# One lo part made by VectorE instead of TensorE, pair 1's weights widened in two steps, two convolution parts moved later, in a fused convolution and squared-ReLU MLP

## The chip, the cores and the metric

The kernel runs on one core of one Trainium2 chip. The metric is device time in microseconds (us), median of three runs: 2234.77 us before the change (2234.75 to 2234.77). The engines are TensorE (PE, with its weight loads PEld), VectorE (DVE), ScalarE (ACT), GpSimd (POOL) and SyncE (SP, which issues the DMAs). Each engine takes its own instructions in the order in which they stand, and waits for the others by semaphores.

## The reference

```
w   = exp(w - max(w)); w = w / (sum(w) + 1e-9)        # 8 heads x 7 taps, softmax over the taps
x   = causal convolution of x (8 x 4096 x 192) with w, head by head (24 channels each)
h   = x @ w_in            # 32768 x 192 @ 192 x 2048
g   = s * relu(h)**2 + b
out = g @ w_out           # 32768 x 2048 @ 2048 x 192
```

All of it is float32. w_in and w_out come to the core as 64-bit floats.

## The kernel before

**Precision.** TensorE works on fp32r, a rounded float32. Every factor is therefore split in a hi part (a cast to fp32r) and a lo part (the value minus its hi part), and a product is the sum of hi*hi, hi*lo and lo*hi. For an activation tile sA, slot 0 is hi and slot 1 is lo; W and WB hold the weights likewise.

**Tiling.** The 32768 tokens are 32 groups n of 1024, and a group is two blocks j of 512. The 192 channels are two parts: A (128 channels) and B (64 channels, those of both blocks stacked in one tile). The 2048 hidden units are eight pairs p of two chunks of 128. `first(n, j, p)` (L522) makes h for one pair: 18 matmuls of 64 rows each, two of which run side by side, with a PSUM tile h of which there are two. `relu` and `square` (L543, L551) on ACT, a cast for the hi part qh on ACT or DVE, and `lows` (L557) on DVE for the lo part ql follow. `second_whole` (n = 0, 10 matmuls) and `second` (later groups, 20 matmuls) multiply qh and ql by w_out and accumulate over the pairs. A queue holds at least two finished (qh, ql) back, so that TensorE runs `first` of later pairs ahead of `second` of earlier ones. At pairs 4 and 6 (`TWICE`) no second runs; pair 7 empties the queue.

**The convolution.** A group's convolution is a chain of small steps for DVE: seven taps (L161, L163) for A of block 0, then its split, seven for B (accB) with its split, and seven for A of block 1. `convolve(k)` (L708) emits the next k of these steps for the coming group; what a call leaves over where a tap chain ends is owed to the next call. For group 0 there is no earlier time: B and A of block 1 are convolved by TensorE with diagonal matrices (`conv_tensor`, L254), A of block 0 by DVE.

**The weights.** A pair's weights are widened from 64-bit words on the chip during group 0 (class `Widen`, L284): `magnitudes` (ACT, one instruction into a tile t, of which there are two), `top` (DVE, three instructions), `his` (ACT casts to the hi parts), `low` (DVE, two) and `los` (DVE, two for each part of the columns). Columns 0 to 383 are w_in of the pair, 384 to 767 its w_out. `fetch(p)` (L346) loads a pair's words by one DMA of 768 KB; there are three tiles of words, so `fetch(4)` waits until pair 1's words have been read.

**The order.** `head()` (L381) writes out the start by hand: group 0's convolution and splits, pair 0's weights (w_in and w_out apart), pair 1's, and the firsts of pairs 0 and 1 for both blocks with their squares, while pairs 2 and 3 are being widened. `pair(p)` (L724) does pairs 2 to 7 of group 0, widening pair p+2 and p+1 beside its own squares, with `CONV[p]` convolution steps of group 1. All of DVE, ACT and PE keep this written order over group 0 (`in_order`, L112; SP in `head` too). `ahead` and `between` in `pair` say how many of the steps come before and between the two blocks' squares. From group 1 on a plain loop over (n, j, p) runs (L777), with nothing of the weights left.

Of the kernel before, what the change touches and what calls it, by code (L numbers as in the profile page):

```python
# [9 lines left out]
F32 = mybir.dt.float32  # L10
F32R = mybir.dt.float32r
I32 = mybir.dt.int32
U32 = mybir.dt.uint32
AF = mybir.ActivationFunctionType
ALU = mybir.AluOpType
AX = mybir.AxisListType

P = 128
BLK = 512
# [1 line left out]

LAG = 2

CONV = (0, 1, 1, 1, 1, 1, 4, 8)

TWICE = (4, 6)

# [10 lines left out]
def conv_attention_then_squared_relu_mlp(  # L38
# [23 lines left out]
    nc = tc.nc  # L62
    D, T = outT.shape
    NPAIR = weights64.shape[0]
    K = taps.shape[2]
# [21 lines left out]
    raw = ctx.enter_context(tc.tile_pool(name="raw", bufs=2))  # L87
# [187 lines left out]
    def w_in(part, p, chunk, rows):  # L275
        return W[rows, p, part, chunk * P : (chunk + 1) * P]
# [4 lines left out]
    def w_outB(f, rows=slice(0, P)):  # L281
        return WB[rows, f // 2, f % 2, :]

    class Widen:  # L284


# [11 lines left out]
                yield (*(WB[:, self.p, :, k * DB : (k + 1) * DB] for k in range(2)), v)  # L298

        def magnitudes(self):  # L300
            self.t = raw.tile([P, CT], I32, name="t")[:, self.lo : self.hi]

            top = words[self.p][:, self.lo : self.hi, 1]
            nc.scalar.activation(self.t.bitcast(F32), top.bitcast(F32), AF.Abs)

        def top(self):
            t, top = self.t, words[self.p][:, self.lo : self.hi, 1]
            nc.vector.tensor_scalar(
                t.bitcast(F32), t.bitcast(F32), TOP_MIN, TOP_MAX, op0=ALU.max, op1=ALU.min
            )  # L310

            nc.vector.tensor_scalar(
                t, t, 3, 0x3FFFFFFF, op0=ALU.logical_shift_left, op1=ALU.bitwise_and
            )
            nc.vector.scalar_tensor_tensor(  # L315
                t, top, -0x40000000, t, op0=ALU.bitwise_and, op1=ALU.bitwise_or
            )
# [28 lines left out]
    def fetch(p, a=0, z=None):  # L346
        if a == 0:
            words[p] = wordp.tile([P, CT, 2], I32, name="words")
        z = z or CT
        nc.sync.dma_start(  # L350
            words[p][:, a:z].rearrange("p f w -> p (f w)"), w_words[p, :, 2 * a : 2 * z]
        )
# [10 lines left out]
    make_identity(nc, ident)  # L363

    nc.scalar.activation(tsum, idle[:, 0:2], AF.Exp)
    nc.vector.reduce_max(tmax, tap, axis=AX.X)
    nc.vector.tensor_tensor(
        tap, tap, tmax.unsqueeze(2).to_broadcast([P, 2, K]), op=ALU.subtract
    )
    nc.scalar.activation(tap, tap, AF.Exp)  # L370
    nc.vector.reduce_sum(tsum, tap, axis=AX.X)
    nc.vector.tensor_scalar(tsum, tsum, 1e-9, None, op0=ALU.add)
    nc.vector.reciprocal(tsum, tsum)
    nc.vector.tensor_tensor(tap, tap, tsum.unsqueeze(2).to_broadcast([P, 2, K]), op=ALU.mult)
# [6 lines left out]
    def head():  # L381


        one = tok[0]

        warm = ps_o.tile([P, BLK], F32, name="acc1")
        for cols in WARM:
            nc.tensor.matmul(
                warm[:, 0:cols], idle, idle[:, 0:1].to_broadcast([P, cols]), start=True, stop=True
            )  # L390
        w0, w0out, w1 = Widen(0, 0, CI), Widen(0, CI, CT), wide[1]

        def diagonal(w):
            d = act.tile([P, 2, BLK], F32, name="q").rearrange("p a (k f) -> p (a k) f", f=P)
            for k in range(K):
                nc.scalar.activation(d[:, k, :], ident, AF.Identity, scale=w[:, k : k + 1])
            return d

        top, bottom = slice(0, DB), slice(DB, P)
        diagB = diagonal(tapB)  # L400
        accB = ps_o.tile([P, BLK], F32, name="acc2")
        acc1 = ps_o.tile([P, BLK], F32, name="acc1")
        one.conv_tensor(accB, diagB, one.xB)
        acc0 = xs.tile([P, BLK], F32, name="accA")
        for _ in one.conv(acc0, one.xA, tapA, BLK):
            pass
        nc.scalar.mul(minus, ident, -1.0)
        diagA = diagonal(tapA)
        w0.magnitudes()
        split = one.split_A(0, acc0)  # L410
        next(split)
        w0.top()
        w0.his()
        tB = one.tB = xs.tile([P, 2, BLK], F32R, name="tB")
        wB = one.wB = xs.tile([P, 2, BLK], F32R, name="wB")
        hiB = xs.tile([P, BLK], F32R, name="hiB", bufs=1)
        lo = one.split_tensor(accB, hiB, lambda: one.conv_tensor(acc1, diagA, one.xA[:, BLK:], range(0, 2)))
        one.conv_tensor(acc1, diagA, one.xA[:, BLK:], range(2, K))
        next(split)
        fetch(2)  # L420
        w1.magnitudes()
        w0.rest()
        w1.top()
        nc.scalar.copy(tB[top, 0, :], hiB[top].bitcast(F32))
        nc.scalar.copy(wB[bottom, 0, :], hiB[top].bitcast(F32))
        lo(tB[bottom, 0, :], top)
        lo(wB[top, 0, :], top)
        w1.his()
        w1.low()
        w0out.magnitudes()  # L430
        w0out.top()
        w1.los()
        nc.scalar.copy(tB[top, 1, :], hiB[bottom].bitcast(F32))

        def second_block():
            sA = one.sA[1] = xs.tile([P, 2, BLK], F32R, name="sA", bufs=3)
            wA = one.wA[1] = xs.tile([P, 2, BLK], F32R, name="wA", bufs=3)
            lo1 = one.split_tensor(acc1, sA[:, 0, :])
            one.swap(wA[:, 0, :], sA[:, 0, :])
            lo(tB[bottom, 1, :], bottom)  # L440
            one.swap(wB[:, 1, :], tB[:, 1, :])
            lo1(sA[:, 1, :], slice(0, P))
            one.swap(wA[:, 1, :], sA[:, 1, :])


        ha = first(0, 0, 0, second_block)
        w0out.his()
        q = relu(ha)
        w0out.rest()
        wide[2].magnitudes()  # L450
        wide[2].top()
        fetch(3)
        start_tokens(1)
        fetch(4)
        ha = first(0, 0, 1)
        a1 = relu(ha)
        queue.append((0, 0, 0, *lows(*square(q, nc.vector.tensor_copy))))
        hb = first(0, 1, 0)
        wide[2].low()
        b0 = squares(hb, nc.scalar.copy)  # L460
        queue.append((0, 1, 0, *lows(*b0)))
        wide[2].his()
        wide[2].los()
        hb = first(0, 1, 1)
        queue.append((0, 0, 1, *lows(*square(a1, nc.scalar.copy))))
        wide[3].magnitudes()
        wide[3].top()
        b1 = squares(hb, nc.scalar.copy)
        wide[3].his()
        queue.append((0, 1, 1, *lows(*b1)))  # L470
        convolve(CONV[1])

    wide = {p: Widen(p, 0, CT) for p in range(1, NPAIR)}
# [48 lines left out]
    def first(n, j, p, meanwhile=None):  # L522
        h = ps_h.tile([P, 2, BLK], F32, name="h")
        halves = [tok[n].half(j, i) for i in range(2)]

        def both(w, part, at, start, stop):

            for i in range(2):
                chunk = halves[i][at]
                rows = slice(i * HB, (i + 1) * HB)  # L530
                nc.tensor.matmul(  # L531
                    h[:, i, :], w_in(w, p, chunk[0], rows), chunk[part], start=start, stop=stop
                )
# [315 lines left out]
```

## Time and profile before

| | |
|---|---|
| median of three runs | 2234.77 us |
| span of the profiled execution (first to last instruction) | 2232.9 us |
| what lies around the span | 1.9 us |
| PE busy | 2226.4 us, 100% of the span |
| DVE busy | 1753.5 us, 79% |
| ACT busy | 1286.4 us, 58% |
| granted TensorE clock | 1.00 in the whole span |
| chain that ended last | PE 98%, DVE 1%, ACT 1% |

The busy share is an average over stages: group 0 takes the first 90 us or so, and in the first four of the page's 40 slices DVE is at 8, 8, 9 and 8 tenths, later mostly at 7. An idle gap on PE before an instruction is shown in brackets with what ended it.

### The profile page before, as it was taken

Reading aid. Unit: us, or ns where it says so; the run is one execution under the profiler, and the core shown is the slowest. Engines: PE = TensorE matmul, PEld = TensorE weight load, DVE = VectorE, ACT = ScalarE, POOL = GpSimd, SP = SyncE. Lnnn points to the kernel's source line nnn. Section 1 sums busy time; section 2 is a strip of 40 time slices with the busy share of each in tenths; the row PEclk is TensorE's granted clock in tenths of the full one; section 3 lists DMA queues with packets and bytes.
Section 4 is the critical chain, followed back from the end, with each engine's and each line's share of the span. In section 5 each row is a group of like instructions: output and inputs, shape, how many; then the busy total and the mean of one; then the engine's idle time right before and its main releaser. Section 6 shows DMA issues by size and latency. Waiting matters only on the chain.

```text
span 2232.9 us, 45081 instructions
## 1 busy us (share of the span) xinstructions
PE 2226.4 (100%) x19330; PEld 1829.1 (82%) x19330; DVE 1753.5 (79%) x1995; ACT 1286.4 (58%) x1410; POOL 317.8 (14%) x205
## 2 busy tenths in 40 slices
PE   9999999999999999999999999999999999999999
PEld 6788888888888888888888888888888888888887
DVE  8898778777787787777877878778777787787764
ACT  8755555655555555555555555555655555556554
POOL 0022101111011011110110111111101111011110
PEclk9999999999999999999999999999999999999999
DMA  5113112121121111211111111112121121111110
GB/s 180 34 43 87 40 46 62 48 58 44 44 58 53 53 44 45 56 53 53 43 51 50 53 53 53 48 43 62 51 55 44 44 58 53 53 44 42 46 39 17
DMA packets 46168, 117.51 MB, mean 53 GB/s; under 512 B 7760, under 2 KB 8016, under 8 KB 45968
## 3 DMA queue, kind: packets, MB, share of 16 engines
q1 hardware_dynamic: 45824, 114.50, 18.6%
q8 instruction: 151, 2.47, 0.5%
q14 instruction: 49, 0.40, 0.1%
q10 hardware_dynamic: 144, 0.13, 0.0%
HBM read 31.64 MB, written 25.17 MB: 25 GB/s over the span
## 4 chain that ended last, share of the span: by engine, by line
PE 98%; DVE 1%; ACT 1%; DMA 0%; issue 0%; SPq 0%; DVEq 0%
PE acc L614 50%; PE h L531 46%; DVE accA L163 0%; PE acc L576 0%; ACT q L552 0%; DVE ql L559 0%; PE acc L577 0%; PE acc L583 0%; PE acc L582 0%; PE acc L581 0%; ACT qh L554 0%; ACT q L545 0%; DMA xA<-in_xA 0%; DVE t L315 0%; ACT oC L589 0%
## 5 line engine op out<-in xcount | busy, mean ns | idle before, releaser
L545 ACT ACTIVATE q<-h 128x1024 f32<-128x1024 f32 x512 | 525.5, 1026 | 902.8 <-PE h L531 900.4
L559 DVE TENSOR_TENSOR ql<-q,qh 128x1024 fp32r<-128x1024 f32 x512 | 656.7, 1283 | 56.3 <-ACT qh L554 2.6
L554 DVE CAST qh<-q 128x1024 fp32r<-128x1024 f32 x497 | 370.1, 745 | 395.7 <-ACT q L552 393.3
L614 PE MATMUL acc<-qh,W 64*128 64x512 f32 x3960 | 609.9, 386 | 0.0
L552 ACT ACTIVATE q<-q 128x1024 f32<-128x1024 f32 x512 | 543.6, 1062 | 15.9
L614 PEld LDWEIGHTS acc<-qh,W 64*128 64x128 f32 x3960 | 370.9, 184 | 77.9
L531 PE MATMUL h<-sA,W 64*128 64x512 f32 x3072 | 432.4, 387 | 0.0
L531 PE MATMUL h<-wA,W 64*128 64x512 f32 x3072 | 431.6, 386 | 0.0
L531 PE MATMUL h<-tB,W 64*128 64x512 f32 x1536 | 429.9, 386 | 0.0
L531 PE MATMUL h<-wB,W 64*128 64x512 f32 x1536 | 429.9, 386 | 0.0
L614 PE MATMUL acc<-ql,WB 64*128 64x512 f32 x1980 | 385.7, 386 | 0.4 <-DVE ql L559 0.4
L614 PE MATMUL acc<-qh,WB 64*128 64x512 f32 x1980 | 385.6, 386 | 0.0
L614 PE MATMUL acc<-ql,W 64*128 64x512 f32 x1980 | 385.5, 386 | 0.0
L638 POOL TENSOR_TENSOR oB<-oB,oB 128x512 f32<-128x512 f32 x61 | 115.2, 1889 | 1672.7 <-ACT oB L637 1672.7
L163 DVE SCALAR_TENSOR_TENSOR accA<-xA,tap,accA 128x512 f32<-128x512 f32 x378 | 341.5, 903 | 6.8
L531 PEld LDWEIGHTS h<-sA,W 64*128 64x128 f32 x3072 | 287.3, 184 | 62.9 <-issue 1.1
L531 PEld LDWEIGHTS h<-wA,W 64*128 64x128 f32 x3072 | 287.8, 184 | 60.4
L531 PEld LDWEIGHTS h<-tB,W 64*128 64x128 f32 x1536 | 282.6, 184 | 40.5 <-issue 0.2
L531 PEld LDWEIGHTS h<-wB,W 64*128 64x128 f32 x1536 | 282.5, 184 | 20.1
L614 PEld LDWEIGHTS acc<-ql,WB 64*128 64x128 f32 x1980 | 185.5, 184 | 40.1 <-DVE ql L559 1.3
L614 PEld LDWEIGHTS acc<-ql,W 64*128 64x128 f32 x1980 | 185.5, 184 | 39.0
L614 PEld LDWEIGHTS acc<-qh,WB 64*128 64x128 f32 x1980 | 185.5, 184 | 38.8
(115 smaller groups left out, 1035.4 us busy)
## 6 DMA issues: line engine op xcount, KB each, us to landing
wA<-sA SPq DMA_DIRECT2D x126, 256.0 KB, 3.6
outT<-oA SPq DMA_DIRECT2D x63, 256.0 KB, 2.0
wB<-tB SPq DMA_DIRECT2D x60, 256.0 KB, 3.4
xA<-in_xA SPq DMA_DIRECT2D x24, 515.0 KB, 3.6
xB<-in_xB SPq DMA_DIRECT2D x32, 259.0 KB, 2.6
oC<-oB SPq DMA_DIRECT2D x61, 128.0 KB, 2.2
outT<-oC SPq DMA_DIRECT2D x60, 128.0 KB, 2.3
words<-in_w SPq DMA_DIRECT2D x7, 768.0 KB, 6.2
```

The lines of the kernel that those rows point to most:

```text
L163: nc.vector.scalar_tensor_tensor(acc, src, w[:, k : k + 1], acc, op0=ALU.mult, op1=ALU.add)
L531: nc.tensor.matmul(h[:, i, :], w_in(w, p, chunk[0], rows), chunk[part], start=start, stop=stop)
L545: nc.scalar.activation(q, h, AF.Relu)
L552: nc.scalar.activation(q, q, AF.Square)
L554: cast(qh, q)
L559: nc.vector.tensor_tensor(ql, q, qh.bitcast(F32), op=ALU.subtract)
L614: nc.tensor.matmul(accs[to + 2 * i], w(f, r), q[r, f % 2, :], start=start and f == 0, stop=stop and f == ends[i],)
L638: nc.gpsimd.tensor_tensor(o[1], o[1], o[3], op=ALU.add)
```

## The change

Five things change, all of them in group 0.

1. The tap softmax: the maximum comes negated, and two ACT exponentials (one for each part) take it as a bias and give the sums as well. A DVE subtraction and a DVE sum are gone.
2. In `head`, ACT casts hiB before W's hi part of pair 0 (`w0.his()` moved behind `split_tensor`).
3. Block 1's first lo part, acc1 minus its hi part: was a matmul with minus the identity between the third and fourth group of `first(0, 0, 0)` and an ACT copy out of PSUM; is one DVE subtraction that reads PSUM, and stands ahead of `first(0, 0, 0)`. The DMAs that swap halves stand in another order.
4. Pair 1's weights: w_in is widened where the whole pair was, w_out later, behind the first three squares, ahead of pair 3's. `fetch(4)` moves behind it. Pair 2's magnitudes and top move behind `first(0, 0, 1)` and the first ql.
5. `CONV` goes from (0, 1, 1, 1, 1, 1, 4, 8) to (0, 0, 0, 1, 1, 1, 5, 9).

```diff
-CONV = (0, 1, 1, 1, 1, 1, 4, 8)
+CONV = (0, 0, 0, 1, 1, 1, 5, 9)
...
         def magnitudes(self):
-            self.t = raw.tile([P, CT], I32, name="t")[:, self.lo : self.hi]
+            t = raws[self.p] = raw.tile([P, CT], I32, name="t")
+            self.t = t[:, self.lo : self.hi]
...
+        def part(self, lo, hi):
+
+            of = Widen(self.p, lo, hi)
+            of.t = raws[self.p][:, lo:hi]
+            return of
...
-    nc.vector.reduce_max(tmax, tap, axis=AX.X)
-    nc.vector.tensor_tensor(
-        tap, tap, tmax.unsqueeze(2).to_broadcast([P, 2, K]), op=ALU.subtract
-    )
-    nc.scalar.activation(tap, tap, AF.Exp)
-    nc.vector.reduce_sum(tsum, tap, axis=AX.X)
+    nc.vector.reduce_max(tmax, tap, axis=AX.X, negate=True)
+    for g in range(2):
+        nc.scalar.activation(
+            tap[:, g, :], tap[:, g, :], AF.Exp, bias=tmax[:, g : g + 1],
+            accum_out=tsum[:, g : g + 1],
+        )
...
         w0.top()
-        w0.his()
...
         lo = one.split_tensor(accB, hiB, lambda: one.conv_tensor(acc1, diagA, one.xA[:, BLK:], range(0, 2)))
+        w0.his()
...
-        w1.magnitudes()
+        wide[1].magnitudes()
+        w1, w1out = wide[1].part(0, CI), wide[1].part(CI, CT)
         w0.rest()
-        w1.top()
...
+        w1.top()
         w1.his()
         w1.low()
+        w1.los()
         w0out.magnitudes()
+        nc.scalar.copy(tB[top, 1, :], hiB[bottom].bitcast(F32))
+        lo(tB[bottom, 1, :], bottom)
+        one.swap(wB[:, 1, :], tB[:, 1, :])
...
+        nc.scalar.copy(sA[:, 0, :], acc1)
+        one.swap(wA[:, 0, :], sA[:, 0, :])
         w0out.top()
-        w1.los()
...
-            lo1 = one.split_tensor(acc1, sA[:, 0, :])
...
-            lo1(sA[:, 1, :], slice(0, P))
...
-        ha = first(0, 0, 0, second_block)
+        nc.vector.tensor_tensor(
+            sA[:, 1, :], acc1, sA[:, 0, :].bitcast(F32), op=ALU.subtract
+        )
+        one.swap(wA[:, 1, :], sA[:, 1, :])
+
+        ha = first(0, 0, 0)
         w0out.his()
         q = relu(ha)
         w0out.rest()
-        wide[2].magnitudes()
-        wide[2].top()
         fetch(3)
         start_tokens(1)
-        fetch(4)
         ha = first(0, 0, 1)
-        a1 = relu(ha)
         queue.append((0, 0, 0, *lows(*square(q, nc.vector.tensor_copy))))
+        a1 = relu(ha)
+        wide[2].magnitudes()
+        wide[2].top()
...
         queue.append((0, 0, 1, *lows(*square(a1, nc.scalar.copy))))
+        w1out.top()
+        w1out.his()
+        w1out.rest()
+        fetch(4)
+        b1 = relu(hb)
         wide[3].magnitudes()
+        b1 = square(b1, nc.scalar.copy)
         wide[3].top()
-        b1 = squares(hb, nc.scalar.copy)
```

The order on ACT about the relu of `first(0, 1, 1)`. q_365 before and q_367 after are that relu's tile; t_262 and t_289 belong to pair 2, t_360 and t_369 to pair 3, t_190 to pair 1.

Before:

```order
L322 CAST W_96<-t_262 128x640
L322 CAST WB_97<-t_262 128x2x64
L552 ACTIVATE q_294<-q_294 128x1024
L554 CAST qh_356<-q_294 128x1024
L304 ACTIVATE t_360<-words_267 128x768
L545 ACTIVATE q_365<-h_336 128x1024
L552 ACTIVATE q_365<-q_365 128x1024
```

After:

```order
L331 CAST W_96<-t_289 128x640
L331 CAST WB_97<-t_289 128x2x64
L565 ACTIVATE q_287<-q_287 128x1024
L567 CAST qh_349<-q_287 128x1024
L331 CAST W_96<-t_190 128x256
L331 CAST WB_97<-t_190 128x2x64
L558 ACTIVATE q_367<-h_329 128x1024
L307 ACTIVATE t_369<-words_257 128x768
L565 ACTIVATE q_367<-q_367 128x1024
```

Two casts of pair 1's w_out now stand ahead of that relu, and pair 3's magnitudes behind it.

The order on DVE at the same place, from the ql of block 1 and pair 0 on (ql_328 before, ql_321 after; ql_358 and ql_351 are block 0 and pair 1).

Before:

```order
L559 TENSOR_TENSOR ql_328<-q_323,qh_326 128x1024
L335 TENSOR_TENSOR W_96<-t_262,W_96 128x640
L335 TENSOR_TENSOR WB_97<-t_262,WB_97 128x2x64
L337 TENSOR_TENSOR W_96<-W_96,c_320 128x640
L337 TENSOR_TENSOR WB_97<-WB_97,c_320 128x2x64
L559 TENSOR_TENSOR ql_358<-q_294,qh_356 128x1024
L308 TENSOR_SCALAR t_360<-t_360 128x768
```

After:

```order
L572 TENSOR_TENSOR ql_351<-q_287,qh_349 128x1024
L317 TENSOR_SCALAR t_190<-t_190 128x384
L321 TENSOR_SCALAR t_190<-t_190 128x384
L324 SCALAR_TENSOR_TENSOR t_190<-words_122,t_190 128x384
L337 TENSOR_SCALAR c_358<-t_190 128x384
L338 SCALAR_TENSOR_TENSOR c_358<-words_122,c_358 128x384
L344 TENSOR_TENSOR W_96<-t_190,W_96 128x256
L344 TENSOR_TENSOR WB_97<-t_190,WB_97 128x2x64
L346 TENSOR_TENSOR W_96<-W_96,c_358 128x256
L346 TENSOR_TENSOR WB_97<-WB_97,c_358 128x2x64
L317 TENSOR_SCALAR t_369<-t_369 128x768
```

Nine instructions on pair 1's w_out now stand between block 0's second ql and pair 3's top.

The order on DVE at the end of group 0, from the ql of block 1 and pair 6 (ql_812 before and ql_817 after are this one) to the split of accB.

Before:

```order
L559 TENSOR_TENSOR ql_812<-q_801,qh_810 128x1024
L163 SCALAR_TENSOR_TENSOR accA_374<-xA_269,tap_58,accA_374 128x512
L180 TENSOR_TENSOR sA_853<-accA_374,sA_853 128x512
L161 TENSOR_SCALAR accB_859<-xB_270,tap_58 128x512
L163 SCALAR_TENSOR_TENSOR accB_859<-xB_270,tap_58,accB_859 128x512 x3
L559 TENSOR_TENSOR ql_869<-q_864,qh_867 128x1024
L163 SCALAR_TENSOR_TENSOR accB_859<-xB_270,tap_58,accB_859 128x512 x2
L559 TENSOR_TENSOR ql_878<-q_873,qh_876 128x1024
L163 SCALAR_TENSOR_TENSOR accB_859<-xB_270,tap_58,accB_859 128x512
L216 TENSOR_TENSOR tB_953<-accB_859,hiB_955 64x512
```

After:

```order
L572 TENSOR_TENSOR ql_817<-q_806,qh_815 128x1024
L163 SCALAR_TENSOR_TENSOR accA_568<-xA_259,tap_58,accA_568 128x512 x3
L180 TENSOR_TENSOR sA_860<-accA_568,sA_860 128x512
L161 TENSOR_SCALAR accB_866<-xB_260,tap_58 128x512
L163 SCALAR_TENSOR_TENSOR accB_866<-xB_260,tap_58,accB_866 128x512 x2
L572 TENSOR_TENSOR ql_875<-q_870,qh_873 128x1024
L163 SCALAR_TENSOR_TENSOR accB_866<-xB_260,tap_58,accB_866 128x512 x2
L572 TENSOR_TENSOR ql_884<-q_879,qh_882 128x1024
L163 SCALAR_TENSOR_TENSOR accB_866<-xB_260,tap_58,accB_866 128x512 x2
L216 TENSOR_TENSOR tB_960<-accB_866,hiB_962 64x512
```

Three taps of accA instead of one stand between that ql and the split of accA, and two taps of accB instead of one between the last ql of group 0 and the split of accB.

## Rows read from the trace of the kernel before

**Rows 1.** The page, first part: busy us (share of the span) and instructions.

```profile
PE 2226.4 (100%) x19330; PEld 1829.1 (82%) x19330; DVE 1753.5 (79%) x1995; ACT 1286.4 (58%) x1410; POOL 317.8 (14%) x205
```

**Rows 2.** Busy time by stretch: us, length, busy by engine (instructions), granted clock, DMA.

```profile
40.00:60.00 20.00, 20.00 (x139) 15.19 (x138) 18.87 (x28) 18.27 (x21) 0.15 (x1) 1.00 0.19 68
...
200.00:300.00 100.00, 100.00 (x886) 82.65 (x884) 79.21 (x89) 55.87 (x61) 14.62 (x9) 1.00 0.22 59
```

**Rows 3.** Timeline of PE: start, us, instruction [idle before <-what ended it], the start.

```profile
12.62 0.51 PE L230 MATMUL acc<-hiB,minus 128*128 128x512 f32 x1 [0.16 <-ACT hiB L227]
...
17.34 0.98 PE L531 MATMUL h<-sA,W 64*128 64x512 f32 x6
...
18.72 0.50 PE L230 MATMUL acc<-sA,minus 128*128 128x512 f32 x1 [0.40 <-ACT sA L227]
...
19.15 0.50 PE L531 MATMUL h<-tB,W 64*128 64x512 f32 x1
...
31.76 0.97 PE L531 MATMUL h<-sA,W 64*128 64x512 f32 x6
...
32.56 0.39 PE L531 MATMUL h<-tB,W 64*128 64x512 f32 x1
...
33.95 0.85 PE L531 MATMUL h<-sA,W 64*128 64x512 f32 x6
```

**Rows 4.** Timeline of DVE, pairs 0 to 3 being widened.

```profile
13.97 0.55 DVE L308 TENSOR_SCALAR t<-t 128x768 f32<-128x768 f32 x1
...
16.15 0.56 DVE L328 TENSOR_SCALAR c<-t 128x768 int32<-128x768 int32 x1
...
17.62 0.35 DVE L308 TENSOR_SCALAR t<-t 128x384 f32<-128x384 f32 x1
...
18.88 0.82 DVE L335 TENSOR_TENSOR W<-t,W 128x640 fp32r<-128x640 f32 x1
...
20.86 0.36 DVE L328 TENSOR_SCALAR c<-t 128x384 int32<-128x384 int32 x1
...
22.81 0.55 DVE L308 TENSOR_SCALAR t<-t 128x768 f32<-128x768 f32 x1
...
28.23 1.22 DVE L559 TENSOR_TENSOR ql<-q,qh 128x1024 fp32r<-128x1024 f32 x1
...
29.36 0.82 DVE L335 TENSOR_TENSOR W<-t,W 128x640 fp32r<-128x640 f32 x1
...
31.24 1.22 DVE L559 TENSOR_TENSOR ql<-q,qh 128x1024 fp32r<-128x1024 f32 x1
...
32.38 0.55 DVE L308 TENSOR_SCALAR t<-t 128x768 f32<-128x768 f32 x1
```

**Rows 5.** Timeline of ACT, the relu of first(0, 1, 1).

```profile
31.73 1.01 ACT L545 ACTIVATE q<-h 128x1024 f32<-128x1024 f32 x1
```

**Rows 6.** Timeline of DVE and PE, pair 5's w_in and its first use.

```profile
53.87 0.81 DVE L337 TENSOR_TENSOR W<-W,c 128x640 fp32r<-128x640 f32 x1
...
54.21 1.03 PE L531 MATMUL h<-sA,W 64*128 64x512 f32 x6
```

**Rows 7.** Timeline of DVE, ACT and PE, the end of group 0.

```profile
72.34 1.03 ACT L545 ACTIVATE q<-h 128x1024 f32<-128x1024 f32 x1 [1.01 <-PE h L531]
...
78.62 0.75 DVE L163 SCALAR_TENSOR_TENSOR accA<-xA,tap,accA 128x512 f32<-128x512 f32 x1
...
79.40 0.62 ACT L178 CAST sA<-accA 128x512 fp32r<-128x512 f32 x1 [1.96 <-DVE accA L163]
...
81.18 2.33 DVE L163 SCALAR_TENSOR_TENSOR accB<-xB,tap,accB 128x512 f32<-128x512 f32 x3
...
88.19 0.62 ACT L209 CAST hiB<-accB 128x512 fp32r<-128x512 f32 x1 [1.95 <-DVE accB L163]
...
97.19 0.50 PE L614 MATMUL acc<-ql,WB 64*128 64x512 f32 x2 [0.35 <-DVE ql L559]
```

**Rows 8.** DMAs of the tile words, from issue to landing.

```profile
DMA to landing us min/median/max: 4.1/5.3/7.9
```

More of the change, by code (lines that the diff above doesn't have):

```diff
@@ L282, in w_outB @@
         return WB[rows, f // 2, f % 2, :]
+    raws = {}
     class Widen:
@@ L390, in head @@
             )
-        w0, w0out, w1 = Widen(0, 0, CI), Widen(0, CI, CT), wide[1]
+        w0, w0out = Widen(0, 0, CI), Widen(0, CI, CT)
         def diagonal(w):
@@ L427, in head @@
         lo(wB[top, 0, :], top)
+        w1.top()
         w1.his()
         w1.low()
+        w1.los()
         w0out.magnitudes()
-        w0out.top()
-        w1.los()
[L433 to L437, printed above, removed]
-            lo1 = one.split_tensor(acc1, sA[:, 0, :])
-            one.swap(wA[:, 0, :], sA[:, 0, :])
-            lo(tB[bottom, 1, :], bottom)
-            one.swap(wB[:, 1, :], tB[:, 1, :])
-            lo1(sA[:, 1, :], slice(0, P))
-            one.swap(wA[:, 1, :], sA[:, 1, :])
-        ha = first(0, 0, 0, second_block)
+        nc.scalar.copy(tB[top, 1, :], hiB[bottom].bitcast(F32))
+        lo(tB[bottom, 1, :], bottom)
+        one.swap(wB[:, 1, :], tB[:, 1, :])
+        sA = one.sA[1] = xs.tile([P, 2, BLK], F32R, name="sA", bufs=3)
+        wA = one.wA[1] = xs.tile([P, 2, BLK], F32R, name="wA", bufs=3)
+        nc.scalar.copy(sA[:, 0, :], acc1)
+        one.swap(wA[:, 0, :], sA[:, 0, :])
+        w0out.top()
+        nc.vector.tensor_tensor(
[3 more added lines that the diff above has]
+        ha = first(0, 0, 0)
         w0out.his()
@@ L449, in head @@
         w0out.rest()
+        fetch(3)
+        start_tokens(1)
+        ha = first(0, 0, 1)
+        queue.append((0, 0, 0, *lows(*square(q, nc.vector.tensor_copy))))
+        a1 = relu(ha)
         wide[2].magnitudes()
         wide[2].top()
-        fetch(3)
-        start_tokens(1)
-        fetch(4)
-        ha = first(0, 0, 1)
-        a1 = relu(ha)
-        queue.append((0, 0, 0, *lows(*square(q, nc.vector.tensor_copy))))
         hb = first(0, 1, 0)
```

## The prediction

> **What bounds the kernel now.** I read the page's busy times first, then the stretches, then the timelines of the engines over group 0. PE is busy for 2226.4 of 2232.9 us [rows 1], and from 200 us on without a gap: 100.00 of 100.00 us, with DVE at 79% and ACT at 56% [rows 2]. So from group 1 on the work runs at PE's own pace, and what is won or lost in group 0 is carried to the end unchanged. Group 0 is another matter: from 40 to 60 us DVE is busy for 18.87 and ACT for 18.27 of 20 us beside a full PE [rows 2]. There the reader is to look not at PE's share but at how much earlier or later a DVE result comes than PE asks for it. That margin is thin. PE waits for pair 5's weights (six matmuls of `first` take 1.03 us at 54.21 where they take 0.85 at 33.95) just as DVE ends them, at 53.87 + 0.81 = 54.68 [rows 3, 6]; and at 97.19 it waits 0.35 us for group 1's first ql [rows 7].
>
> **The start: about 1.8 us won.** The lo part by PE sits inside `first(0, 0, 0)`. From the first six matmuls to the next group takes 19.15 - 17.34 = 1.81 us, and 32.56 - 31.76 = 0.80 us where nothing stands between, so 1.0 us goes [rows 3]. ACT's cast of hiB comes out ahead of a cast of W: PE's wait of 0.16 us at 12.62, with the restart behind it up to 0.4, goes too [rows 3]. The softmax loses one DVE instruction before and one after the exponentials and gains one ACT instruction; no row here prices an exponential with a sum, so I put it between 0.3 us lost and 0.3 won for PE, and take 0.3. Together 1.0 + 0.4 + 0.3 = 1.7 to 1.8 us (bounds 0.9 to 1.8). DVE wins nothing by it, since its next work waits for data.
>
> **DVE's chain up to pair 1's squares.** In the blocks below every duration is from the start of a block to the start of the next [rows 4]. Of 768 columns `top` takes 16.15 - 13.97 = 2.18, `low` 17.62 - 16.15 = 1.47, `los` 31.24 - 29.36 = 1.88 us. Of 384 columns `top` takes 18.88 - 17.62 = 1.26, `low` and `los` together 22.81 - 20.86 = 1.95. A ql takes 32.38 - 31.24 = 1.14. A piece that waits for the piece just before it costs some 0.1 more.
>
> Until 13.97 DVE's order is as before. Then come pair 1's w_in, 1.26 + 1.95 + 0.1 = 3.3 (17.3); pair 0's w_out top, 1.26 (18.55); the new subtraction. That one reads PSUM, which no row of DVE near it shows: as half of a ql it is 0.6, and at most a whole one, 1.14; I take 0.6 (19.15). Then pair 0's w_out, 1.95 (21.1); the cast and ql of the first square with pair 2's top and low, before in another order 28.23 - 22.81 = 5.42, with waits between them 5.8 (26.9); the ql of block 1, 1.14, ready at 28.1. PE, 1.8 us early, has finished four firsts of 2.05 and ten matmuls of the first `second` by about 27.4, and waits 0.7 there: the first part of the gain is gone.
>
> **The new wait.** Now pair 2's los, 1.88, a ql, 1.14, and then pair 1's w_out top, 1.26 + 0.1: 28.1 + 4.4 = 32.5. Only then can ACT make the two hi casts of that w_out, and the relu of `first(0, 1, 1)` is queued behind them on ACT, where before it ran at 31.73 with nothing of DVE ahead of it [rows 5]. Casts 0.5 and relu 1.0: h is free at 34.0. There are two tiles h, so `first(0, 1, 2)` starts at 34.05; before it started at 33.95 [rows 3]. All of the 1.8 us is spent. What else is queued behind: pair 3's magnitudes on ACT (0.9), so pair 3's top on DVE starts at 34.9 instead of 32.38 [rows 4], 2.5 us late.
>
> **Pairs 2 to 5.** Two convolution parts are taken out here: at most 0.75 each as the L163 of rows 7 has it, less for the plain first tap; I take 1.1 for both (bounds 1.0 to 1.5). The rest of DVE's order is the same, and with DVE at 94% [rows 2] nothing else gives time back. So DVE is 2.5 - 1.1 = 1.4 us late where it ends pair 5's w_in: 54.68 becomes 56.0 to 56.1. PE was already waiting for that, so it becomes late by the same: 1.3 to 1.4 us. Bounds: nothing, if idle DVE time that I can't see takes it up, and 1.9 with the dearer subtraction (0.5 more).
>
> Splitting a pair in two is not free: top 2 x 1.26 - 2.18 = 0.34, the rest 2 x 1.95 - 1.47 - 1.98 (18.88 to 20.86) = 0.45, 0.8 us in all by rows 4. It is inside the chain above. [...]
>
> **The end of group 0.** At 72.34 ACT waits for PE [rows 7], so there all are late by PE's 1.35. From the ql of block 1 and pair 6 on, three taps of accA stand where one stood, and a tap that waits for the one before costs 2.33 / 3 = 0.78 [rows 7]. ACT's split of accA (79.40) is queued ahead of the relu of `first(0, 0, 7)`, which PE has long finished: ACT sits idle 1.96 us for DVE already [rows 7]. So 2 x 0.78 = 1.55 more comes straight on ACT's chain, which runs without a gap from 79.40 to the last cast of group 0. Behind the last ql two taps of accB stand where one stood: 0.78 more, and hiB (88.19), for which ACT waits 1.95 [rows 7], is late by 1.35 + 1.55 + 0.78 = 3.7. Behind hiB on ACT stand the casts for tB and wB, four copies of outputs and the relu of `first(1, 0, 0)`; behind that relu the square, DVE's cast and ql(1, 0, 0). PE waits for that ql now, so all 3.7 us reach it at 97.19 [rows 7]. On the way it waits in pieces: for ql of pair 7 (its margins are about 1 us and 0.5), for wB, for that ql.
>
> **Sum.** Won 1.8, lost again by the end of pair 1; +1.35 at pair 5; +1.55 and +0.78 at the end: +3.7 us. The span becomes 2232.9 + 3.7 = 2236.6 us, and with the 1.9 us around it, as between this span and the median shown, 2238.5. That is 0.16% slower; a difference under 0.2%, 4.5 us, counts as none here.
>
> **The rivals.**
>
> 1. *Pairs 1 to 5 stay ahead.* DVE's lag is taken up, and PE keeps its 1.8 us to 72.34. Then only the taps count: -1.8 + 2.33 = +0.5, 2235.3 us. For it: PE's lead is real and shown by rows. Against it: rows 2 leave 1.1 us of idle DVE time in 20, and the wait on ACT is one of order, which no speed takes away. 10%.
>
> 2. *The taps are hidden too*, since ql(1, 0, 0) was not the only thing PE waited for: -1.8, 2233.0 us. Against it: ACT's two long waits in rows 7 are for just these taps. 2%.
>
> 3. *Slower beyond the bound: the words of pair 4 come late.* `fetch(4)` now waits until pair 1's w_out has been read, at about 33.5, and SyncE issues its loads in order. A load of words lands in 4.1 to 7.9 us [rows 8], at 37.6 to 41.4; ACT wants to read them at about 41.0, behind the cast of qh(0, 0, 2). So up to 7.5 us it costs nothing, then one for one, since ACT's relu of block 1 stands behind it. At 9 us it would be 1.5: 3.7 + 1.5 = 5.2, 2240.0 us. The loads of group 2 no longer run beside it ahead of it, which speaks against. 7%.
>
> 4. *The start alone counts*, if the subtraction out of PSUM were four times as dear as I take it: 1.8 later in DVE's chain, 3.7 + 1.8 = 5.5, 2240.3 us. 2%.
>
> **Chances and range.** The forecast has 79%; within it the lag at pair 5 (0.9 to 1.9) and the tap step (0.75, its own length, to 0.78) give 2237.9 to 2239.0. Down to 2236.5 it takes in part of the way to rival 1, up to 2239.7 part of that to rival 3. Slower by over 4.5 us: rivals 3 and 4 and a little of the forecast's own upper end, 11%. Faster by over 4.5 us: no case reaches it, 1%. The rest, 88%, is within the bound.
>
> **What would show it.** In the new profile: six matmuls of `first(0, 0, 0)` followed by the next group within 0.8 us, and a start of it near 16.5; ACT idle for about 3 us before the cast of pair 1's w_out, and PE waiting about 1.4 us for the relu behind it; pair 3's top near 34.9; pair 5's w_in done near 56.1, with PE waiting; ACT's cast of hiB near 91.9; PE's wait for ql(1, 0, 0) ending near 100.9. I am wrong if the cast of pair 1's w_out does not hold up the relu, if PE does not wait around 55 us, or if hiB comes less than 3 us later than before.

## The result and the profile after

The changed kernel takes 2238.76 us (median of 17 runs, 2238.39 to 2239.80), the kernel before, beside it, 2234.93 (17 runs, 2234.46 to 2235.40). That is 3.83 us more, a ratio of 1.0018 with a 95% interval of 1.0011 to 1.0025, so the two are less than 0.2% apart by the median. The profiled execution of the changed kernel took 2239.07 us, with a span of 2237.3 us against 2232.9: 4.4 us. By the medians the forecast of +3.7 is 0.1 off, by the two profiles 0.7. The 0.7 is what there is to explain: it is a difference between two single executions, and the profiled one of before was about 0.2 us under its median, that of the changed kernel 0.3 over.

The page's first part, and stretches of 13 and 20 us (us, length, busy by engine, granted clock, DMA):

```profile
PE 2228.3 (100%) x19329; PEld 1829.6 (82%) x19329; DVE 1756.6 (79%) x2001; ACT 1286.2 (57%) x1413; POOL 317.9 (14%) x205
```

```profile
27.00:40.00 13.00, 11.69 (x66) 8.43 (x65) 12.44 (x22) 9.70 (x15) 0.00 (x0) 1.00 0.55 196
40.00:60.00 20.00, 19.30 (x133) 14.51 (x133) 18.76 (x29) 19.75 (x23) 0.15 (x1) 1.00 0.24 79
60.00:80.00 20.00, 20.00 (x125) 15.71 (x123) 18.14 (x27) 15.87 (x19) 0.00 (x0) 1.00 0.00 1
80.00:100.00 20.00, 19.10 (x104) 14.83 (x104) 14.05 (x19) 13.87 (x17) 0.00 (x0) 1.00 0.16 40
```

The shares of the whole span [rows 1] move by a point at most. The stretches do move: PE was full from 27 to 60 us (40 to 60 in [rows 2]) and lacked 0.35 us of 20 from 80 to 100; now the gaps are 1.3, 0.7 and 0.9 us in three stretches: about 34 us, about 56, and from 88 on. The timeline shows each. First the start (start, us, instruction, idle before and what ended it): two lines of the kernel before, then PE and DVE of the changed one:

```profile
4.51 6.22 PE L257 MATMUL acc<-xB,q 128*128 128x512 f32 x14
...
26.87 0.50 PE L576 MATMUL acc<-qh,WB 128*128 128x512 f32 x1
```

```profile
4.59 6.82 PE L257 MATMUL acc<-xB,q 128*128 128x512 f32 x14
...
17.57 0.96 PE L544 MATMUL h<-sA,W 64*128 64x512 f32 x6
18.37 0.39 PE L544 MATMUL h<-tB,W 64*128 64x512 f32 x1
...
26.00 0.50 PE L589 MATMUL acc<-qh,WB 128*128 128x512 f32 x1
...
18.75 0.68 DVE L450 TENSOR_TENSOR sA<-acc,sA 128x512 fp32r<-128x512 f32 x1
...
22.11 0.69 DVE L567 CAST qh<-q 128x1024 fp32r<-128x1024 f32 x1 [0.74 <-ACT q L565]
22.84 1.22 DVE L572 TENSOR_TENSOR ql<-q,qh 128x1024 fp32r<-128x1024 f32 x1
```

The first six matmuls are followed after 0.80 us where it was 1.81 [rows 3], so the 1.0 us is gone. But they begin at 17.57, not at 16.5, later even than before. The first `second` (L589, before L576) starts 0.87 us earlier than before. And DVE, which had no wait there, now waits 0.74 us for the first square. Next the new wait at pair 1, on ACT, PE and DVE:

```profile
33.16 0.41 ACT L331 CAST W<-t 128x256 fp32r<-128x256 f32 x1 [3.03 <-DVE t L324]
33.47 0.29 ACT L331 CAST WB<-t 128x128 fp32r<-128x128 f32 x1
33.67 1.02 ACT L558 ACTIVATE q<-h 128x1024 f32<-128x1024 f32 x1
...
34.74 0.98 PE L544 MATMUL h<-sA,W 64*128 64x512 f32 x6 [1.21 <-ACT q L558]
...
35.51 0.56 DVE L317 TENSOR_SCALAR t<-t 128x768 f32<-128x768 f32 x1 [0.32 <-ACT t L307]
```

ACT stands idle for 3.03 us, and the relu queued behind the casts comes at 33.67 instead of 31.73 [rows 5]. At pair 5:

```profile
55.86 0.82 DVE L346 TENSOR_TENSOR W<-W,c 128x640 fp32r<-128x640 f32 x1
...
56.73 0.50 PE L544 MATMUL h<-sA,W 64*128 64x512 f32 x2 [0.64 <-DVE W L346]
```

DVE ends pair 5's w_in at 56.68 (before 54.68 [rows 6]), 2.0 us late, and PE waits for it in the middle of six matmuls. And the end of group 0, on ACT, DVE and PE:

```profile
74.33 1.03 ACT L558 ACTIVATE q<-h 128x1024 f32<-128x1024 f32 x1 [1.01 <-PE h L544]
...
80.61 2.32 DVE L163 SCALAR_TENSOR_TENSOR accA<-xA,tap,accA 128x512 f32<-128x512 f32 x3
...
82.96 0.62 ACT L178 CAST sA<-accA 128x512 fp32r<-128x512 f32 x1 [3.53 <-DVE accA L163]
...
90.97 1.53 DVE L163 SCALAR_TENSOR_TENSOR accB<-xB,tap,accB 128x512 f32<-128x512 f32 x2
92.54 0.62 ACT L209 CAST hiB<-accB 128x512 fp32r<-128x512 f32 x1 [2.74 <-DVE accB L163]
...
91.11 0.50 PE L590 MATMUL acc<-ql,WB 128*128 128x512 f32 x1 [0.55 <-DVE ql L572]
...
98.47 0.96 PE L544 MATMUL h<-sA,W 64*128 64x512 f32 x6 [0.26 <-ACT q L558]
...
101.55 0.51 PE L627 MATMUL acc<-ql,WB 64*128 64x512 f32 x2 [0.50 <-DVE ql L572]
```

Set beside [rows 7], one reads a staircase: at the relu +1.99 us (74.33 - 72.34), at accA's cast +3.56, at hiB's +4.35, and where PE's wait for ql(1, 0, 0) ends +4.36. The steps between are 1.57 (two taps) and 0.79 (one tap). ACT's waits for taps grow from 1.96 and 1.95 by the same. Nothing is added after that: the span is 4.4 longer.

### The profile page after: what moved, and what is told of

Same layout as the page of the kernel before. It is cut to its first block, busy times and chain, and to the rows that moved or that the text cites. A ratio compares the mean times of both kernels' runs of the same rounds, so it can differ in the third digit from the quotient of the medians.

```text
span 2237.3 us, 45089 instructions
## 1 busy us (share of the span) xinstructions
PE 2228.3 (100%) x19329; PEld 1829.6 (82%) x19329; DVE 1756.6 (79%) x2001; ACT 1286.2 (57%) x1413; POOL 317.9 (14%) x205
## 4 chain that ended last, share of the span: by engine, by line
PE 97%; DVE 2%; ACT 1%; issue 0%; DVEq 0%; POOL 0%; POOLq 0%
PE acc L627 50%; PE h L544 45%; PE acc L257 1%; DVE ql L572 0%; ACT q L565 0%; ACT q L558 0%; ACT qh L567 0%; PE acc L397 0%; DVE accA L163 0%; DVE t L324 0%; DVE c L338 0%; DVE W L344 0%; DVE t L321 0%; DVE qh L567 0%; PE acc L589 0%
```

## The experiments

The theory: two costs add up, DVE's lag at pair 5 and the three taps behind it, and the lag has two parts, the new order at pair 1 and a start that is worth less than forecast. The main rivals: only one of the two costs reaches the end; the split or the queue on ACT is what costs; the start is lost or kept whatever DVE does. Each number stands beside the kernel before of its own chip, since that moves by 0.3 us from one to the next (2234.63 to 2234.93); the changed kernel's own +3.83 is the mark. The 95% interval of each ratio reaches about 0.0009, or 2 us, to either side. A difference of less than that between two variants therefore rests on the traces and not on the medians, and each kernel has one trace.

| kernel | median us (11 runs) | before | difference |
|---|---|---|---|
| before, new CONV alone | 2236.66 | 2234.66 | +2.00 |
| changed, old CONV | 2237.35 | 2234.66 | +2.69 |
| changed, old softmax | 2239.15 | 2234.66 | +4.49 |
| changed, pair 1 whole | 2237.55 | 2234.66 | +2.89 |
| changed, relu ahead of the casts | 2238.27 | 2234.63 | +3.64 |
| before, lo part by VectorE alone | 2234.84 | 2234.63 | +0.21 |
| before, relu of pair 7 first, other CONV | 2234.18 | 2234.63 | -0.45 |
| the same, lo part by VectorE | 2234.57 | 2234.63 | -0.06 |
| before, PE later by a matmul | 2235.11 | 2234.71 | +0.40 |
| changed, PE later by a matmul | 2239.95 | 2234.71 | +5.24 |

### The taps: the new CONV alone

```diff
-CONV = (0, 1, 1, 1, 1, 1, 4, 8)
+CONV = (0, 0, 0, 1, 1, 1, 5, 9)
```

> The kernel before with the new CONV alone. Theory: two costs add up in the changed kernel, a lag at pair 5 (1.98 us in its trace) and three taps on the chain at the end of group 0 (2.35). Here the lag is gone, and DVE is even about 1.1 us earlier at pair 5, so that PE's small wait there goes (0.2 to 0.4 won); the taps cost their 2.35. Expected 1.9 to 2.2 us slower than before, 2236.8 to 2237.1, with the last cast of hiB of group 0 at 90.1 to 90.3 (before 88.19). Rival 1, the taps are hidden and the lag alone is what cost time: 0 to 0.4 faster, 2234.5 to 2234.9. Rival 2, the end alone is what cost time, whatever stands before it: 3.8 slower, 2238.7.

Measured +2.00 us. Its timeline, DVE at pair 5 and ACT at the end of group 0:

```profile
53.00 0.82 DVE L337 TENSOR_TENSOR W<-W,c 128x640 fp32r<-128x640 f32 x1
...
72.14 1.03 ACT L545 ACTIVATE q<-h 128x1024 f32<-128x1024 f32 x1 [1.01 <-PE h L531]
...
80.77 0.62 ACT L178 CAST sA<-accA 128x512 fp32r<-128x512 f32 x1 [3.53 <-DVE accA L163]
...
90.34 0.62 ACT L209 CAST hiB<-accB 128x512 fp32r<-128x512 f32 x1 [2.74 <-DVE accB L163]
```

Pair 5 is 0.87 us earlier than before and PE 0.20 ahead at 72.14; then come 1.57 and 0.78, and hiB is 2.15 late. The taps are on the chain, by their own length, with no lag ahead of them.

### The lag: the changed kernel with the old CONV

```diff
-CONV = (0, 0, 0, 1, 1, 1, 5, 9)
+CONV = (0, 1, 1, 1, 1, 1, 4, 8)
```

> The changed kernel with the old CONV. Theory: the three taps at the end (2.35 us) go, but two parts come back in pairs 1 and 2, so that pair 5's w_in is 0.6 to 1.1 later still than in the changed kernel (56.68 there): about 57.3 to 57.8, PE late by 2.6 to 3.1 there and by nothing more at the end. Expected 2.5 to 3.0 us slower than before, 2237.4 to 2237.9, and ACT's waits for accA and accB near 1.96 each as before the change. Rival 1, the taps are hidden: slower than the changed kernel, 2239.4 or more. Rival 2, the taps alone cost time and the lag is made up for behind pair 5: within 0.3 of before, 2235.

Measured +2.69 us. The same places, and PE's and DVE's first steps:

```profile
16.91 0.96 PE L544 MATMUL h<-sA,W 64*128 64x512 f32 x6
...
22.18 1.23 DVE L572 TENSOR_TENSOR ql<-q,qh 128x1024 fp32r<-128x1024 f32 x1
...
74.34 1.03 ACT L558 ACTIVATE q<-h 128x1024 f32<-128x1024 f32 x1 [1.01 <-PE h L544]
...
81.39 0.62 ACT L178 CAST sA<-accA 128x512 fp32r<-128x512 f32 x1 [1.95 <-DVE accA L163]
...
90.17 0.62 ACT L209 CAST hiB<-accB 128x512 fp32r<-128x512 f32 x1 [1.95 <-DVE accB L163]
```

Late by 2.00 at 74.34 and by 1.98 at 90.17: behind pair 5 nothing is added and nothing made up. ACT's waits for the taps are 1.95 again. Pair 5's w_in was expected 0.6 to 1.1 us later than in the changed kernel; it ends at 56.67 (56.68 there). This profile is 2.0 us late and the median 2.69; the profiled execution started 0.66 us earlier than that of the changed kernel (16.91 against 17.57), and its first ql came 0.66 earlier too. The eleven times stand in two groups, four from 2236.64 to 2236.85, the profiled one among them, and seven from 2237.33 to 2238.05. That pointed to the start.

### The order on ACT: the relu ahead of the casts

```diff
         w1out.top()
+        b1 = relu(hb)
         w1out.his()
         w1out.rest()
         fetch(4)
-        b1 = relu(hb)
         wide[3].magnitudes()
```

> The changed kernel with the relu of first(0,1,1) moved ahead of the two casts of pair 1's w_out on ACT; DVE's order is as it was. Theory: PE's time in group 0 is set by DVE's chain, which ends pair 5's w_in at 56.68 in the changed kernel; the wait on ACT at 34.7 is only the first place where that is seen. So PE's wait of 1.2 us at 34.7 goes, PE waits longer at pair 5 instead, and only what DVE gains by an earlier pair 3 counts (its top waits 0.32 for ACT there): 0.3 to 0.5 us under the changed kernel's 2238.76, 2238.2 to 2238.5. Rival (the forecast's own step): the wait in ACT's order is what cost the lead, so all of its 1.2 us is won, 2237.5.

Measured +3.64, 0.19 better than the changed kernel beside its own before (0.49 by the bare medians; in the two profiles 0.52 where ACT waits for PE at 74 us, of which 0.09 is an earlier start, 17.48 against 17.57). The relu now comes at 29.92 and PE's wait at 34.7 is gone, but PE comes to pair 5 early and stands there (ACT, then PE):

```profile
29.92 1.02 ACT L558 ACTIVATE q<-h 128x1024 f32<-128x1024 f32 x1
...
54.83 0.73 PE L544 MATMUL h<-sA,W 64*128 64x512 f32 x4 [0.34 <-ACT q L558]
...
56.21 0.50 PE L544 MATMUL h<-sA,W 64*128 64x512 f32 x2 [0.65 <-DVE W L346]
```

It waits at 56.21 where the changed kernel waits at 56.73. The rival, that the queue on ACT is what costs the lead, would have given 1.2 us. The wait on ACT is the first place where a late DVE shows, and taking it away moves the wait on to the next.

### The split: pair 1 widened whole

```diff
-        w1, w1out = wide[1].part(0, CI), wide[1].part(CI, CT)
+        w1 = wide[1]
...
-        w1out.top()
-        w1out.his()
-        w1out.rest()
         fetch(4)
```

> The changed kernel with pair 1 widened whole, in one step, where its w_in was (fetch(4) behind the second square's ql as there). Theory: the casts of pair 1's w_out no longer stand ahead of the relu of first(0,1,1) on ACT, so PE's wait of 1.2 us at 34.7 goes, and the 0.8 us that the split costs DVE; pair 5's w_in is then 1.5 to 1.8 earlier (near 55.0), and only the taps at the end are left: 1.4 to 1.8 us under the changed kernel, 2237.0 to 2237.4. Rival 1, only the split's own 0.8 us goes, since pair 0's w_out and the first squares wait instead: 2238.0. Rival 2, the order at pair 1 is without effect behind pair 5: 2238.8.

Measured +2.89: 0.9 us won (1.2 by the bare medians) where 1.4 to 1.8 were expected. Half of the reasoning held. PE and DVE in its timeline:

```profile
22.79 0.96 PE L541 MATMUL h<-sA,W 64*128 64x512 f32 x6 [0.81 <-ACT q L555]
...
30.65 0.50 PE L587 MATMUL acc<-ql,WB 128*128 128x512 f32 x1 [0.33 <-DVE ql L569]
...
53.88 0.82 DVE L346 TENSOR_TENSOR W<-W,c 128x640 fp32r<-128x640 f32 x1
```

DVE ends pair 5's w_in at 54.70, as before the change, and 1.98 us earlier than in the changed kernel. But PE has new waits, at 22.79 for the first relu (queued on ACT behind pair 0's w_out, which DVE widens later here) and at 30.65 for a ql. Where ACT waits for PE, 72.34 before, this run is at 73.29, still 0.95 late. The split is dear, and it also bought something: it brings those two forward.

### The start: the old softmax

```diff
-    nc.vector.reduce_max(tmax, tap, axis=AX.X, negate=True)
-    for g in range(2):
-        nc.scalar.activation(
-            tap[:, g, :], tap[:, g, :], AF.Exp, bias=tmax[:, g : g + 1],
-            accum_out=tsum[:, g : g + 1],
-        )
+    nc.vector.reduce_max(tmax, tap, axis=AX.X)
+    nc.vector.tensor_tensor(
+        tap, tap, tmax.unsqueeze(2).to_broadcast([P, 2, K]), op=ALU.subtract
+    )
+    nc.scalar.activation(tap, tap, AF.Exp)
+    nc.vector.reduce_sum(tsum, tap, axis=AX.X)
```

> The changed kernel with the old tap softmax. In the trace of the changed kernel each exponential with a sum is two instructions, the taps' diagonals start 0.12 us later, PE's fourteen matmuls of the convolution of B take 6.82 us (6.22 before) with weight loads of 0.25 us at their start, and DVE then waits 0.74 for the first square. Theory: the later diagonals leave PE idle a moment longer behind its warm-up, and the first of these matmuls run at the slower rate; with the old softmax they take 6.2 again, first(0,0,0) starts near 16.8 (17.57), DVE's wait is under 0.2, pair 5's w_in ends near 56.0, and the time is 0.5 to 0.7 under the changed kernel's 2238.76: 2238.1 to 2238.3. Rival, the 0.6 us is chance of one execution, or a lead of PE at the start is lost anyway: the same 2238.8 within 0.2.

Measured +4.49, nothing won: the theory that the softmax makes the start late fell. (The median is 0.66 over the changed kernel's +3.83, less than the intervals can tell; the two spans, 2237.4 and 2237.3, are alike.) PE in its timeline:

```profile
4.56 6.95 PE L257 MATMUL acc<-xB,q 128*128 128x512 f32 x14
...
17.68 0.96 PE L544 MATMUL h<-sA,W 64*128 64x512 f32 x6
```

The fourteen matmuls take 6.95 us with the old softmax too. What the softmax itself costs is read between the first instruction on the landed taps and the first diagonal: 1.53 us in three profiles with the old one (before, this one, new CONV alone), 1.65 or 1.66 in three with the new one (changed, old CONV, pair 1 whole). The new one loses 0.13 us. ACT in the changed kernel, the exponential of the first part:

```profile
2.73 0.30 ACT L377 ACTIVATE tap<-tap,tmax 128x7 f32<-128x7 f32 x1 [0.51 <-DVE tmax L375]
2.94 0.19 ACT L377 ACTIVATION_READ_ACCUMULATOR tap<-tap,tmax 128x1 f32 x1
```

Over all twelve profiles the fourteen matmuls take 6.22 to 7.30 us, under 6.3 in three of them, among these the profile of before and that of the changed kernel with the old CONV. Whether they are long or short goes with no edit: the kernel before and the one with the new CONV alone have the same instructions up to there, and take 6.22 and 7.12.

### The start: PE made later by one matmul, in both kernels

```diff
         one.conv_tensor(accB, diagB, one.xB)
+        nc.tensor.matmul(warm, diagB[:, 0, :], one.xB[:, 0:BLK], start=True, stop=True)
```

> The kernel before with one matmul more (a first tap of B, 128x512 in float32, 0.86 us, into the warm-up's tile) between the convolutions of B and of A's block 1, so that PE comes to first(0,0,0) later. Theory: in the order before, DVE reaches the first square's ql by its own work (25.62 us, and 25.65 in the run with the new CONV alone, where first(0,0,0) started 0.51 us later), so a later PE costs little: 0 to 0.4 us, 2234.6 to 2235.0. Rival: PE is busy 100% of the span, so each us more at its start is a us more at its end: 2235.5.

> The changed kernel with the same matmul more. Theory: in the changed order DVE waits for the first square, so PE's start stands on DVE's chain: in three traces of that order DVE's first ql starts 5.27 us after first(0,0,0), whether that starts at 16.91 or at 17.68. So the 0.86 us reach pair 5 and the end one for one: 2238.76 + 0.86 = 2239.6, with DVE's wait for the first square near 1.6 us. Rival (the forecast's view): what PE wins or loses at the start is taken up by pair 1's wait, which DVE alone sets: 2238.8.

Measured +0.40 on the kernel before, and 5.24 - 3.83 = +1.41 on the changed one. In the kernel before, first PE, then DVE and ACT:

```profile
18.38 0.96 PE L532 MATMUL h<-sA,W 64*128 64x512 f32 x6
...
26.18 1.23 DVE L560 TENSOR_TENSOR ql<-q,qh 128x1024 fp32r<-128x1024 f32 x1
...
72.88 1.03 ACT L546 ACTIVATE q<-h 128x1024 f32<-128x1024 f32 x1 [1.02 <-PE h L532]
```

and in the changed one, with DVE between:

```profile
18.90 0.96 PE L545 MATMUL h<-sA,W 64*128 64x512 f32 x6
...
24.17 1.23 DVE L573 TENSOR_TENSOR ql<-q,qh 128x1024 fp32r<-128x1024 f32 x1
...
75.67 1.03 ACT L559 ACTIVATE q<-h 128x1024 f32<-128x1024 f32 x1 [1.02 <-PE h L545]
```

In the old order a `first(0, 0, 0)` that starts 1.04 us later (18.38 against 17.34) costs 0.54 at 72 us. In the new order 1.33 us later costs 1.33 at DVE's first ql and 1.34 at 75.67: one for one. (It is 1.33 and not the 0.86 of the extra matmul (11.19 to 12.05 in the kernel before with it) because this execution's fourteen took 7.30 us. The +1.41 of the medians is more than 0.86 too; the changed kernel did not run beside this one, and what the rest is stays open.) In the changed order DVE's first ql comes 5.27 us after `first(0, 0, 0)` starts, in all four profiles read for it: 16.91 to 22.18, 17.57 to 22.84, 17.68 to 22.95, 18.90 to 24.17. In the order before it follows in part at most: 17.34 to 25.62, with the new CONV alone 17.85 to 25.65, with the extra matmul 18.38 to 26.18.

### The lo part alone, and a better version

The kernel before with block 1's lo part on VectorE, and none of the other four parts of the change. What stood inside `first(0, 0, 0)` stands ahead of it, and pair 0's w_out top behind pair 1's los:

```diff
-        w0out.top()
...
+        w0out.top()
+        nc.vector.tensor_tensor(
+            sA[:, 1, :], acc1, sA[:, 0, :].bitcast(F32), op=ALU.subtract
+        )
+        one.swap(wA[:, 1, :], sA[:, 1, :])
...
-        ha = first(0, 0, 0, second_block)
+        ha = first(0, 0, 0)
```

> The kernel before with block 1's first lo part made by VectorE alone (pair 1 whole, old CONV, old softmax, old order of the casts). Theory: PE gains the 1.0 us of the matmul with minus the identity inside first(0,0,0), but DVE has 0.61 us more work in the stretch where it ends last, and ACT's casts of pair 0's w_out wait longer for DVE ahead of the first relu; so PE loses the lead by 30 us and ends 0.1 to 0.4 us later than before, 2234.8 to 2235.1 against a before of 2234.66. Rival: work taken off a PE that is busy 100% of the span is won, 1.0 us: 2233.7.

Measured +0.21, no difference that the runs can tell. One us of work was taken off PE; PE gives back 0.74 of it in one wait, for the first relu, which stands on ACT behind pair 0's w_out and so behind DVE:

```profile
22.35 0.96 PE L530 MATMUL h<-sA,W 64*128 64x512 f32 x6 [0.74 <-ACT q L544]
```

Then, without any lo part on VectorE, the end of group 0 was taken up where the staircase is:

```diff
-CONV = (0, 1, 1, 1, 1, 1, 4, 8)
+CONV = (0, 0, 1, 1, 1, 2, 4, 8)
...
-        convolve(ahead)
         def magnitudes():
...
         qa = relu(ha)
+        convolve(ahead)
```

> The kernel before with two edits: in pair 7 the relu of block 0 stands ahead of the four convolution steps instead of behind them, and CONV is (0, 0, 1, 1, 1, 2, 4, 8). Theory: at the end of group 0 the taps cost time only because ACT's cast of accA is queued ahead of that relu; with the relu first, and one part moved from pair 1 to pair 5, where DVE waits 0.5 us, PE has no wait left after 20 us (the waits of 0.2 at pair 5 and of 0.35 at 97 us go, with the restarts behind them): 0.6 to 0.9 us faster than before, 2233.8 to 2234.1. Rival: ACT's wait for the taps moves behind the relu and the later accA is the next wait: no change, 2234.7 within 0.2.

Measured -0.45 beside its before (2233.85 to 2234.54 against 2234.30 to 2235.07), less than expected. The ratio's interval, 0.9989 to 1.0007, does not exclude no change; it has the lowest median of all kernels here. ACT's wait for accA is 1.03 instead of 1.96, that for accB 2.75 instead of 1.95. The stretch from 80 to 100 us, 19.65 before, is full, and that from 40 to 60 stays full (ACT, then the stretches):

```profile
71.91 1.02 ACT L545 ACTIVATE q<-h 128x1024 f32<-128x1024 f32 x1 [1.02 <-PE h L531]
...
78.96 0.62 ACT L178 CAST sA<-accA 128x512 fp32r<-128x512 f32 x1 [1.03 <-DVE accA L163]
```

```profile
40.00:60.00 20.00, 20.00 (x140) 15.43 (x139) 18.28 (x28) 18.03 (x21) 0.15 (x1) 1.00 0.16 56
...
80.00:100.00 20.00, 20.00 (x130) 16.00 (x131) 15.48 (x22) 15.91 (x19) 0.00 (x0) 1.00 0.21 53
```

Not all of this comes from the relu. In the two profiles this version is 0.23 us ahead at DVE's first ql (25.39 against 25.62), where neither edit has acted yet and DVE's first tap began 0.23 earlier (4.83 against 5.06, a wait for the load of xA). It is 0.43 ahead at 71.91, ahead of pair 7, 0.44 at accA's cast, and 0.71 at hiB's (87.48). What the two edits are worth each was not run apart.

Last, the lo part by VectorE on top of that, with hiB's cast and the first relu moved ahead of W's casts on ACT:

```diff
-        w0.his()
...
+        w0.his()
...
+        nc.vector.tensor_tensor(
+            sA[:, 1, :], acc1, sA[:, 0, :].bitcast(F32), op=ALU.subtract
+        )
+        one.swap(wA[:, 1, :], sA[:, 1, :])
+        w0out.top()
...
-        ha = first(0, 0, 0, second_block)
+        ha = first(0, 0, 0)
+        q = relu(ha)
         w0out.his()
-        q = relu(ha)
```

> The kernel relu7 with block 1's first lo part made by VectorE (the subtraction ahead of pair 0's w_out top on DVE), ACT's cast of hiB ahead of W's, and the first relu ahead of the casts of pair 0's w_out. Theory: PE starts 1.5 us earlier, but DVE's 0.61 us stand ahead of the first two ql of group 0, on the chain; PE waits there and comes out 0.6 us behind relu7: 2234.4 to 2234.7. Rival: with no wait of PE left in relu7 the earlier start is kept, 1.0 us or more faster than relu7: 2232.9.

Measured 2234.57, 0.39 behind that version on the same chip, and not 1.0 ahead. In the profiles `first(0, 0, 0)` starts at 17.68 against 17.30, and DVE's ql of block 1 and pair 0 at 28.55 against 27.99: 0.56 later, near the 0.61 that the subtraction takes there; DVE does not wait ahead of its first square, so the later start of PE is not what delays it. The 0.39 itself is less than the medians can tell from none.

## Why the prediction was right, and where it was not

Right, with their size:

- The lo part inside `first(0, 0, 0)`: 1.0 us gone, as forecast. The wait for hiB with its restart: from the end of the fourteen matmuls (start plus length) to `first(0, 0, 0)` it is 6.16 us instead of 6.61, so 0.45 gone, forecast 0.4. The subtraction out of PSUM: 0.61 us from its start to the next one's (18.75 to 19.36), forecast 0.6. Rival 4 (four times that) falls.
- The order at pair 1: ACT idle 3.03 us (forecast about 3), the relu queued behind the casts, PE waiting 1.21 (1.4). But the forecast spoke of the gain as spent by this wait. The run with the relu moved ahead shows that it would have been spent at pair 5 anyway; what spends it is the longer list that DVE works through ahead of pair 5's w_in.
- The taps: 1.57 and 0.79 in place of 1.55 and 0.78, straight on ACT's chain, with and without a lag ahead of them. Rivals 1 and 2 fall, since PE waits at 56.73, and hiB is later by every tap.
- The words of pair 4 (rival 3) came in time: ACT reads them at 41.63 us, with no idle time in front.

Wrong is the first term of the sum, "Together 1.0 + 0.4 + 0.3 = 1.7 to 1.8 us (bounds 0.9 to 1.8)". The first `second` starts at 26.00 instead of 26.87: 0.87 us won, just under the lower bound, and the wait of 0.7 forecast in the middle of that `second` is 0.1. Two pieces failed. The softmax, put at 0.3 won between 0.3 lost and 0.3 won, loses 0.13. And the profile of before was one of the three in twelve in which the first fourteen matmuls are short (6.22 us); in the changed kernel's profile they take 6.82, 0.6 more. Where both are short (changed kernel, old CONV) `first(0, 0, 0)` starts at 16.91, that is 0.43 earlier; with the 1.0 us behind it 1.4 are won.

With it fell the sentence "DVE wins nothing by it, since its next work waits for data", which was true but left out the other sign. Pair 2's top stood ahead of the first square on DVE and now stands behind it, so DVE comes to that square first and waits. So what PE loses at the start, DVE loses, and pair 5 is late by 2.0 instead of 1.35. With the start of the old-CONV run, 0.66 us earlier, it would be 2.00 - 0.66 = 1.34, the forecast's number; this last subtraction is arithmetic, not a run. The runs with one matmul more show the rule behind it. The miss is carried along: pair 3's top, pair 5's w_in, hiB and the end of PE's wait for ql(1, 0, 0) were forecast at 34.9, 56.1, 91.9 and 100.9 us and come at 35.51, 56.68, 92.54 and 101.55, each 0.6 or 0.65 late.

The sum: -0.87 at the start, +1.99 at pair 5, +3.56 and +4.35 at the end in the profiles; +3.83 by the medians. That the medians meet the forecast within 0.1 us is in part luck, since its first term missed by 0.9 in the profiles, and no run shows which start a median execution had. The changed kernel's times spread over 1.4 us, those of before over 0.9, as one would expect where the start hangs on chance and is carried to the end; that link is argued, not shown.

The split of pair 1 takes DVE 3.30 us for w_in (14.19 to 17.49) and 3.32 for w_out (31.78 to 35.10: its last instruction starts at 34.90, and elsewhere the next follows such a one after 0.20), against 5.52 whole (14.32 to 19.84 in that run): 1.1 us dearer, where the forecast had 0.8 and 0.1 for each wait. The two subtractions of 128x512 take the same 0.68 us here, L450 (at 18.75) out of PSUM and L180 (at 11.66) out of SBUF.

## What to carry to other kernels

PE at 100% of the span says nothing of a stage in which another engine delivers just in time: a us of PE's work moved to such an engine brought nothing here in two runs (the medians were 0.2 and 0.4 us higher, less than the runs can tell). Before work is moved later, look at what its result is queued ahead of on the next engine: the three taps cost their full length (1.57 and 0.79 us) where ACT's cast of them stands ahead of a relu that is long ready. That this order is the only cause is argued, since no run put the relu first with the new CONV; the version with the lowest median does so with the taps nearly as before. Before a gain at the start is put into a sum, see in more than one execution whether that start is stable, and whether the new order makes another engine wait for it.

## What the runs showed of the hardware that was not expected

- An exponential with a sum is two instructions on ACT: an ACTIVATE of 0.30 us and an ACTIVATION_READ_ACCUMULATOR of 0.19, and the taps' two parts need two of each. That undoes the two DVE instructions of 0.17 us which it saves.
- TensorE's pace at the start differs between executions of the same instructions. The weight loads between the first matmuls are at first up to 0.34 us long and then 0.19 us, the first of 0.19 listed at 5.00 us in the profile of before and at 6.98 in that of the changed kernel with one matmul more (with the new CONV alone two of them start 0.86 us apart, at 5.42 and 6.28, and 0.43 apart at 6.80 and 7.23). In the three profiles read in short stretches around that time (before, changed, changed with the old CONV) the granted clock reads 1.00 on both sides of it, so that row does not show it, and PE is busy without a gap from 1.00 us to their end (6.4 or 8 us). No run here shows what decides the time.
